# Scoring 32 queries against 96 keys in 64x32 array tiles instead of 64 queries against 128 keys

## The chip, the cores and the metric

The kernel runs on one core of a Trainium2 chip. The metric is the device time of one execution in microseconds (us), and less is better. The median of three timed runs of the kernel before is 952.88 us.

## The reference

Two layers are computed one after the other. The first is attention with a causal window: a query at position i sees the keys at positions i-63 to i. The second is a gated expert layer on the normalised result.

```
attention: q, k, v (8 batches, 8 heads, 576 positions, 64 wide)
  scores = q k^T / sqrt(64); kept where 0 <= i - j < 64, else -1e9
  attn   = exp(scores - max); attn /= sum + 1e-9
  out    = attn v
expert layer: x = out as (4608 tokens, 512)
  xn = x / sqrt(mean(x^2) + 1e-6) * rms_g
  result = (silu(xn w_gate) * (xn w_val)) w_out          # 512 -> 1536 -> 512
```

## The kernel before

The work is cut in two ways that run interleaved. The attention is done by head pairs: 8 batches of 4 pairs, so pairs 0 to 31. The expert layer is done by tiles of 512 tokens, t = 0 to 8, and its matmuls (f16, in a high and a low part) are most of what TensorE does. While TensorE works on the expert layer of one batch, the attention of the batches after it is slipped in between.

Pairs 0 to 7 go through an older path in the first 145 us, where the order of every engine is written out by hand in the string `ORDER` (names such as `g.p_7_0_1` stand for "the next GpSimd instruction that writes p_7_0_1"). Pairs 8 to 31 are done in whole-pair visits, and these alone are changed. A planner places them: `visit_at` says at which half step a visit falls, `at_slot` and `after` place the smaller pieces in slots (one slot is six 512-column or twelve 256-column matmuls of the expert layer), and the resulting order of every engine is fixed.

Visit n does two things on TensorE, one right after the other:

- It multiplies the weights of pair n-2 with its values (`attention_values`): 16 matmuls in 128x64 array tiles, and for the first query block two matmuls in 64x64 tiles, which are held back in the list `ahead` and run together with the scores.
- It computes the scores of pair n (`products_of_pair`): 16 matmuls in 64x64 array tiles, each 64 queries (the weights) against 128 keys (the moving columns), and two matmuls of 64 columns for the first query block, which has no block before it. All are float32, and the trace shows each such matmul as two passes. The four 64x64 tiles of the array ("corners") get one matmul each in turn. Head 0 writes one PSUM bank, head 1 another, and the first block goes into a free part of the bank `first` of the values.

Then, in `scores_of_pair`, VectorE adds the mask and takes the minimum (9 instructions, one per unit of 128 rows), ScalarE takes the exponential with its sum (9), and VectorE takes the reciprocal. `move` then has GpSimd scale each 32x32 block and put it where a 32x32 transpose needs it: 16 instructions for a pair, each 32 partitions by 9 (or 8) units of 32 columns. `turn` has VectorE transpose the blocks (3 instructions), and two visits later TensorE reads the result. Scores, moved blocks and transposed weights share one tile of 8.75 KB a partition: `p` from its start and `m` up to its end, from a rotating pool of three that the weight staging uses as well (`big`).

Of the kernel before, what the change touches and what calls it, by code (L numbers as in the profile page):

```python
# [134 lines left out]
v.p_7_0_0 v.wt16 t.pv_0_8*2 s.p_7_0_0 t.pv_0_8 v.th_0_8 s.mp_o_1 t.pv_0_8 s.st_o_3 t.pv_0_8*5 s.mp_o_2 t.pw_o_1_1*2  # L135
t.pw_o_1_0*2 s.p_7_0_0 t.tr_6_1_1*2 v.wt15 t.pv_0_9 s.mp_1_5 t.pv_0_9*2 v.st_7_0 t.pv_0_9 v.st_7_0 v.th_0_8 t.pv_0_9
g.p_7_0_0 t.pv_0_9 s.pt_6_1_1 t.pv_0_9 v.wt15 t.pv_0_9 s.mn_1_5 t.pv_0_9 v.h_0_4 t.pv_0_9 s.st_o_4 t.pv_0_9*2 g.h_0_4
t.pw_1_5_0 s.mp_o_1 t.pw_1_5_0 t.pw_1_5_1 v.wt13 t.pw_1_5_1 t.pg_0_7*2 g.p_7_0_0 s.mp_o_3 v.wt13 t.pg_0_7 g.p_7_0_1
t.pg_0_7*2 v.th_0_9 t.pg_0_7 s.st_o_5 g.ssq_1 t.tr_7_0_0*2 s.th_0_7 v.top_5 t.tr_7_0_0 t.xp_6_1*7 s.h_0_4 t.xp_6_1
t.pv_0_7*2 s.mn_o_3 t.pv_0_7 v.sq_5 s.kv_9 v.pt_7_0_0 g.h_0_4 t.pv_0_7 v.th_0_7 t.pv_0_7 s.kv_9 t.pv_0_7 t.n2_5 v.z_5  # L140
s.kv_9 s.xb_1 t.pv_0_7 v.ws_5 t.pv_0_7 v.pt_7_0_0 s.wt10 t.pv_0_7 v.wt13 t.pv_0_7*3 v.wt11 t.tr_7_0_1*2 s.kv_6
# [6 lines left out]
t.tr_7_1_0*2 g.p_7_1_1 v.wt19 t.pw_o_5_1*2 s.th_0_11 t.pv_0_10 v.wt19 t.pv_0_10*3 v.pt_7_1_0 t.pv_0_10 s.mp_o_5  # L148
t.pv_0_10 t.pv_0_11*4 v.hsc t.pv_0_11 v.hsc v.omx*2 t.pv_0_11 t.obound v.oe t.tr_7_1_1 v.oe*2 t.tr_7_1_1 v.oe
t.pv_0_11 v.oe v.os v.hsc s.pt_7_1_1 t.pv_0_11 v.th_0_10 t.pv_0_11 s.wt12 t.pv_0_11*3 t.xp_7_1*3 s.h_0_5 t.xp_7_1*3  # L150
v.wt12 t.xp_7_1*2 t.sc_8*3 s.xb_1 t.sc_8*3 g.h_0_5 t.sc_8*2 s.wt13 t.sc_8*8 t.x0_8*2 v.th_0_11 s.kv_7 v.th_0_11 s.wt14
v.ssq_1 v.pm_8 v.hsc v.wt13 v.wt14 s.wt15 v.wt15 s.wt16 v.pm_8 s.wt17 v.wt16 s.h_0_5 v.wt17 g.h_0_5
"""


# [1 line left out]
def tile_window_attention_moe(  # L157
# [369 lines left out]
    def move(m, p, rs, k, qq):

        us = NBLK - 1 if k > 1 else NBLK
        if True:  # L530
            fr, to = slice(32 * qq, 32 * qq + 32), slice(32 * k, 32 * k + 32)
            r = rs[fr, :us].rearrange("p (a b) -> p a b", b=1).to_broadcast([32, us, 32])
            nc.gpsimd.tensor_tensor(m[to, :us, fr], p[fr, :us, to], r, ALU.mult)

    def turn(p, m, part):
        if part < 2:
# [32 lines left out]
    def products_of_pair(n, qk, first, ahead):  # L569

        qt, kk = qk
        sc = [
            pool.tile([P, TT], F32, tag=tag, name=f"sc_{n}_{h}").rearrange("p (i k) -> p i k", k=P)
            for h, (pool, tag) in enumerate(((ps_sc, "sc"), (ps_tr, "tr")))
        ]

        def whole(i, h, par):
            quarter(sc[h][par * D : (par + 1) * D, i, :], qt, kk, h, 2 * i + 1 + par)

        def start(h):  # L580
            quarter(first[h * D : (h + 1) * D, :D], qt, kk, h, 0)

        corners = [[], [], [], []]
        corners[0] = ahead[:1] + [partial(start, 0)] + [partial(whole, i, 0, 0) for i in range(4)]
        corners[1] = ahead[1:] + [partial(whole, i, 0, 1) for i in range(4)]
        corners[2] = [partial(start, 1)] + [partial(whole, i, 1, 1) for i in range(4)]
        corners[3] = [partial(whole, i, 1, 0) for i in range(4)]
        while any(corners):
            for steps_of in corners:
                if steps_of:  # L590
                    steps_of.pop(0)()
        return n, sc, first

    def scores_of_pair(n, sc, first):

        p, m = big(n)
        st = wk.tile([P, 3, NBLK], F32, tag="st", name=f"st_{n}", bufs=NST)
        order = [0] + [u for h in range(2) for u in units(0, h) + units(1, h) if u]
        place = {u: sc[h][:, 2 * g + i, :] for g in range(2) for h in range(2) for i, u in enumerate(units(g, h)) if u}

        def mask_of(u):
            w, v = P if u else D, slot(u)
            masked(p[:, v, :w], place[u] if u else first[:, :D], blocked[:, :P] if u else blocked[:, P:],
                   st[:, 0, v : v + 1])

        def weight_of(u):
            w, v = P if u else D, slot(u)
            weigh(p[:, v, :w], st[:, 0, v : v + 1], st[:, 1, v : v + 1])

        def finish():  # L610
            nc.vector.tensor_scalar(st[:, 1, :], st[:, 1, :], 1e-9, None, ALU.add)
            nc.vector.reciprocal(st[:, 2, :], st[:, 1, :])

        whole[n] = p, m, st[:, 2, :]
        by = MASK_BY if n >= RUSH else 0.5
        for i, u in enumerate(order):
            after(MASK_AT + by * i, partial(mask_of, u))
            after(MASK_AT + by * i + WEIGH, partial(weight_of, u))
        after(MASK_AT + by * NBLK + WEIGH, finish)
# [94 lines left out]
    def attention(b):  # L714

        pairs, soft = {}, {}
        norm = {}

        qs = {}

        def load_queries(hp):
            qs[hp] = load_q(b * NPAIR + hp)

        def load_keys(hp):
            pairs[hp] = load_kv(b * NPAIR + hp)

        def score(hp, g):
            soft[hp, g] = scores(b * NPAIR + hp, g, (qs[hp], pairs[hp][0]))

        def products(hp, first, ahead):  # L730
            return products_of_pair(b * NPAIR + hp, (qs[hp], pairs[hp][0]), first, ahead)

        def moved(hp, k, qq):
            p, m, rs = whole[b * NPAIR + hp]
            move(m, p, rs, k, qq)

        def turned(hp, part):
            p, m, _ = whole[b * NPAIR + hp]
            turn(p, m, part)
            if part == 2:  # L740
                del whole[b * NPAIR + hp]
                soft[hp, 0] = soft[hp, 1] = p

        def to_keys(hp, g):
            soft[hp, g] = weights_to_keys(b * NPAIR + hp, g, soft[hp, g])

        def values(hp, g, xp=None, held=None):
            n = b * NPAIR + hp
            vv = pairs[hp][1]
            p = soft.pop((hp, g))  # L750
            if isinstance(p, list):
                place = {u: p[h][:, i, :] for h in range(2) for i, u in enumerate(units(g, h))}
                at = place.get
            else:
                at = lambda u: p[:, slot(u), :]
            xp = attention_values(n, g, at, vv, xp, held)
            if b >= TB:
                return xp
            drain(hp, g, xp)

        def drain(hp, g, xp):
            n = b * NPAIR + hp
            if hp == g == 0:
                norm["x"] = wk.tile([P, NPAIR, S], F32, tag="xb", name=f"xb_{b}", bufs=1)
                norm["ssq"] = wk.tile([P, S], F32, tag="ssq", name=f"ssq_{b}", bufs=1)
            xb, ssq = norm["x"], norm["ssq"]
            a, z = ((0, XSPLIT), (XSPLIT, S))[g]
            nc.scalar.copy(xb[:, hp, a:z], xp[:, : z - a])
            if g == 0:
                return  # L770
            if b < TB:
                squares(hp, False)
                squares(hp, True)
            else:
                after(1, partial(squares, hp, False))
                after(2, partial(squares, hp, True))

        def squares(hp, add_up):
            n = b * NPAIR + hp
            xb, ssq = norm["x"], norm["ssq"]  # L780
            x2 = pairs[hp][0] if hp else ssq
            if add_up and hp:
                add = nc.vector if (E('ADD', 'ppvppv')[3 * b + hp - 1] == 'v' if b < 2 else hp == NPAIR - 1) else nc.gpsimd
                add.tensor_tensor(ssq, ssq, x2, ALU.add)
            if add_up:
                return
            x2e = E("X2E", "a" * 8)[n] if n < 8 else "a"
            if x2e == "a":
                nc.scalar.activation(x2, xb[:, hp, :], AF.Square)
            else:  # L790
                (nc.vector if x2e == "v" else nc.gpsimd).tensor_tensor(x2, xb[:, hp, :], xb[:, hp, :], ALU.mult)

        return load_queries, load_keys, score, to_keys, values, moved, turned, products, drain, norm

    def attention_events(b, start, pace, tags):
# [10 lines left out]
        for hp in range(NPAIR):  # L806
            if b >= TB:
# [718 lines left out]
```

## Time and profile before

| | |
|---|---|
| timed runs | 952.78, 952.88, 953.68 us |
| span of the profiled execution, first to last instruction | 950.2 us |
| time of the profiled execution beside its span | not given apart from the three runs |
| TensorE busy | 936.1 us, 99% of the span |
| VectorE busy | 625.7 us, 66% |
| ScalarE busy | 510.5 us, 54% |
| GpSimd busy | 497.8 us, 52% |
| granted TensorE clock | 1.000 over the span |

PE is TensorE's matmul, PEld its weight load, DVE VectorE, ACT ScalarE, POOL GpSimd. A busy share counts the modelled end of a matmul, so TensorE's own pace is read from the starts of neighbouring matmuls, not from the busy share. A row of the timeline gives the start of the first instruction of a group, the time from there to the end of its last one, the shape (rows*columns of the array tile, then partitions x moving columns) and the count.

### The profile page before, as it was taken

The numbers are of one execution on the slowest core, as the hardware profiler recorded it, in microseconds if no ns is written. First come the engines' busy times: TensorE is split into PE (matmuls) and PEld (weight loads), VectorE is DVE, ScalarE is ACT, GpSimd is POOL, SyncE is SP. The second block draws the span as 40 slices with busy tenths as digits, with TensorE's granted clock in tenths as the row PEclk, the third lists the DMA queues.
The fourth block names the chain that finished last, engine by engine and source line by source line (L and its number), as shares of the span: only waits on it lengthen the run. The fifth ranks groups of instructions, "written<-read, shape, count | busy, mean of one in ns | idle before, by whom it ended". The sixth has DMA issues, their size and how long they took to land.

```text
span 950.2 us, 20930 instructions
## 1 busy us (share of the span) xinstructions
PE 936.1 (99%) x7906; PEld 614.2 (65%) x7916; DVE 625.7 (66%) x1721; ACT 510.5 (54%) x1303; POOL 497.8 (52%) x641
## 2 busy tenths in 40 slices
PE   8899999999999999999999999999999999999998
PEld 5555554444454444888478857885688568848865
DVE  6998779778877776566857665776676555503540
ACT  7789985555445553566456645664465245413530
POOL 3355545978486773677467747674776122201210
PEclk9999999999999999999999999999999999999999
DMA  8675661515434651457246734564365226614300
GB/s 291 210 224 172 211 194 50 161 43 152 129 90 158 198 193 57 152 206 260 84 139 217 253 103 135 186 257 135 88 207 182 87 70 199 210 44 133 112 12 34
DMA packets 81316, 143.44 MB, mean 151 GB/s; under 512 B 25792, under 2 KB 38336, under 8 KB 81216
## 3 DMA queue, kind: packets, MB, share of 16 engines
q1 hardware_dynamic: 80640, 140.93, 45.1%
q8 instruction: 62, 1.02, 0.4%
q10 hardware_dynamic: 576, 1.18, 0.4%
q14 instruction: 38, 0.31, 0.1%
HBM read 121.64 MB, written 20.45 MB: 150 GB/s over the span
## 4 chain that ended last, share of the span: by engine, by line
PE 89%; DVE 6%; POOL 2%; ACT 1%; issue 1%; DMA 1%; DVEq 0%; POOLq 0%; ACTq 0%
PE bk L182 52%; PE po L182 9%; PE pv L182 7%; PE pg L182 7%; PE xp L182 3%; PE pg L212 3%; PE sc L182 2%; PE pv L212 2%; DVE wt L212 1%; POOL pm L182 1%; PE rb L182 1%; PE sc L212 1%; PE xp L212 1%; DVE p L212 1%; DVE th L182 1%
## 5 line engine op out<-in xcount | busy, mean ns | idle before, releaser
L182 PEld LDWEIGHTS <-wt 128*128 128x128 f16 x3624 | 353.1, 98 | 109.7 <-issue 4.6
L182 POOL TENSOR_TENSOR pm<-pm,st 32x288 f32<-32x288 f32 (+1 forms) x384 | 266.6, 694 | 63.0 <-DVE st L182 19.8
L182 PEld LDWEIGHTS <-h 128*128 128x128 f16 x1308 | 126.7, 98 | 141.6 <-issue 3.3
L182 PE MATMUL bk<-xn,wt 128*128 128x256 f16 x1728 | 207.3, 273 | 0.6 <-DVE u L182 0.5
L182 PE MATMUL bk<-wt,h 128*128 128x512 f16 (+1 forms) x900 | 191.1, 371 | 0.0
L182 POOL TENSOR_TENSOR h<-th,h 128x512 f16<-128x512 f32 x78 | 93.6, 1201 | 169.5 <-ACT h L182 155.6
L182 PE MATMUL bk<-wt,wt 128*128 128x256 f16 x1224 | 150.4, 273 | 0.3 <-ACT u L182 0.3
L182 ACT ACTIVATE pm<-pm,st 128x128 f32<-128x128 f32 (+1 forms) x216 | 83.9, 389 | 37.7 <-DVE st L182 37.0
L182 PE MATMUL po<-wt,h 128*128 128x512 f16 x408 | 90.9, 379 | 0.2 <-DVE wt L212 0.2
L182 ACT CAST h<-th 128x512 f16<-128x512 f32 x94 | 58.0, 617 | 51.7 <-DVE th L182 51.6
L182 POOL TENSOR_TENSOR xn<-xb,xn 128x448 f16<-128x448 f32 (+7 forms) x45 | 37.8, 848 | 83.5 <-ACT xn L182 81.1
L182 DVE SCALAR_TENSOR_TENSOR th<-th,bk 128x256 f32<-128x256 f32 x108 | 44.8, 415 | 49.6 <-ACT th L182 49.2
L182 ACT ACTIVATE th<-bk,hsc 128x256 f32<-128x256 f32 x108 | 48.0, 472 | 46.6 <-DVE bk L182 28.4
L182 DVE TENSOR_TENSOR bk<-bk,s 128x512 f32<-128x512 f32 x36 | 25.1, 696 | 68.8 <-PE bk L182 48.4
L182 PE MATMUL pv<-xn,wt 128*128 128x512 f16 x288 | 66.5, 379 | 0.0
L182 PE MATMUL pg<-xn,wt 128*128 128x512 f16 x288 | 66.1, 379 | 0.0
L182 ACT ACTIVATE ot<-bk,hsc 128x512 f32<-128x512 f32 (+1 forms) x25 | 16.8, 670 | 61.8 <-PE bk L182 61.8
L182 DVE CUSTOM_DVE_ANT_0 pm<-sc,blocked 128x128 f32<-128x128 f32 x191 | 48.8, 282 | 0.0
L182 DVE SCALAR_TENSOR_TENSOR th<-bk,th 128x256 f32<-128x256 f32 x108 | 45.8, 424 | 3.7
L212 PEld LDWEIGHTS <-wt 128*128 128x128 f16 x288 | 27.9, 99 | 31.4 <-issue 0.5
L182 ACT CAST xn<-xb 128x448 f16<-128x448 f32 (+7 forms) x56 | 23.8, 430 | 39.2 <-DVE xb L182 39.1
L182 DVE STREAM_TRANSPOSE pm<-pm 128x512 f32<-128x512 f32 (+1 forms) x72 | 39.6, 554 | 7.9 <-POOL pm L182 7.9
(179 smaller groups left out, 1328.1 us busy)
## 6 DMA issues: line engine op xcount, KB each, us to landing
wt<-sevens SPq DMA_DIRECT2D x108, 512.0 KB, 5.2
kv<-kv SPq DMA_DIRECT2D x28, 608.0 KB, 4.8
wt<-sevens SPq DMA_DIRECT2D x36, 256.0 KB, 2.9
q<-q SPq DMA_DIRECT2D x28, 288.0 KB, 3.7
kv<-kv SPq DMA_DIRECT2D x56, 128.0 KB, 5.0
out<-ot SPq DMA_DIRECT2D x27, 256.0 KB, 2.1
st<-w_gate SPq DMA_DIRECT2D x6, 1024.0 KB, 5.2
st<-w_val SPq DMA_DIRECT2D x6, 1024.0 KB, 5.1
```

The lines of the kernel that those rows point to most:

```text
L182: return real(*args, **kw)
L212: steps[name].popleft()()
```

## The change

The visit's scores are computed in finer pieces. A 64x32 array tile takes 32 queries against the 96 keys that these can see, so each unit of 128 rows has 96 columns instead of 128. That makes 32 matmuls for 16, and five for two in the first block. The eight tiles get one each in turn; the two held-back value matmuls come first. `big` keeps its three tiles for good, sets the four blocks that are never written to zero once, and one small block again at each visit. `move` issues 12 block moves and two for a single unit. The transposes are due 1.6 slots earlier from pair 12 on. A second mask, `banned`, is built once by 16 small GpSimd instructions placed in `ORDER`.

```diff
-t.pw_1_5_0 s.mp_o_1 t.pw_1_5_0 t.pw_1_5_1 v.wt13 t.pw_1_5_1 t.pg_0_7*2 g.p_7_0_0 s.mp_o_3 v.wt13 t.pg_0_7 g.p_7_0_1
+t.pw_1_5_0 s.mp_o_1 t.pw_1_5_0 t.pw_1_5_1 v.wt13 t.pw_1_5_1 t.pg_0_7*2 g.p_7_0_0 s.mp_o_3 v.wt13 t.pg_0_7 g.p_7_0_1 g.banned*16
...
-v.wt12 t.xp_7_1*2 t.sc_8*3 s.xb_1 t.sc_8*3 g.h_0_5 t.sc_8*2 s.wt13 t.sc_8*8 t.x0_8*2 v.th_0_11 s.kv_7 v.th_0_11 s.wt14
-v.ssq_1 v.pm_8 v.hsc v.wt13 v.wt14 s.wt15 v.wt15 s.wt16 v.pm_8 s.wt17 v.wt16 s.h_0_5 v.wt17 g.h_0_5
+v.wt12 t.xp_7_1*2 t.sc_8*6 s.xb_1 t.sc_8*6 g.h_0_5 t.sc_8*4 s.wt13 t.sc_8*16 t.x0_8*5 v.th_0_11 s.kv_7 v.th_0_11 s.wt14
+v.ssq_1 g.pm_8*4 v.pm_8 v.hsc v.wt13 v.wt14 s.wt15 v.wt15 s.wt16 v.pm_8 s.wt17 v.wt16 s.h_0_5 v.wt17 g.h_0_5
...
+    Q = D // 2
+    W3 = 3 * Q
+    banned = cp.tile([P, 2, W3], BF16, name="banned")
+    def band_masks():
...
     def big(n):
-        t = wk.tile([P, ST], I32, tag="st8", name=f"pm_{n}", bufs=NST).bitcast(F32)
-        return (t[:, a : a + NBLK * P].rearrange("p (j k) -> p j k", k=P) for a in (0, ST - NBLK * P))
+        fresh = len(kept_pm) < NST
+        if fresh:
+            kept_pm.append(wk.tile([P, ST], I32, tag="st8", name=f"pm_{n}", bufs=NST).bitcast(F32))
+        t = kept_pm[(n - NPAIR * TB) % NST]
+        p, m = (t[:, a : a + NBLK * P].rearrange("p (j k) -> p j k", k=P) for a in (0, ST - NBLK * P))
+        for qq in range(4) if fresh else (1,):
+            k = (qq + 3) % 4
+            us = slice(0, NBLK if fresh else 1)
+            nc.gpsimd.memset(m[Q * k : Q * k + Q, us, Q * qq : Q * qq + Q], 0.0)
+        return t[:, : NBLK * W3].rearrange("p (j k) -> p j k", k=W3), p, m
...
-    def move(m, p, rs, k, qq):
-        us = NBLK - 1 if k > 1 else NBLK
-        if True:
-            fr, to = slice(32 * qq, 32 * qq + 32), slice(32 * k, 32 * k + 32)
-            r = rs[fr, :us].rearrange("p (a b) -> p a b", b=1).to_broadcast([32, us, 32])
-            nc.gpsimd.tensor_tensor(m[to, :us, fr], p[fr, :us, to], r, ALU.mult)
+    MOVES_OF = 14
+    def move(m, s, rs, step):
+        if step < 12:
+            kk, qq = divmod(step, 4)
+            k, us = (qq + kk) % 4, slice(0, NBLK - 1 if qq == 1 else NBLK)
+        else:
+            kk = k = step - 12
+            qq, us = 1, slice(NBLK - 1, NBLK)
...
-        corners = [[], [], [], []]
-        corners[0] = ahead[:1] + [partial(start, 0)] + [partial(whole, i, 0, 0) for i in range(4)]
-        corners[1] = ahead[1:] + [partial(whole, i, 0, 1) for i in range(4)]
-        corners[2] = [partial(start, 1)] + [partial(whole, i, 1, 1) for i in range(4)]
-        corners[3] = [partial(whole, i, 1, 0) for i in range(4)]
+        def whole(i, h, qq):
+            s = 4 * i + 2 + qq
+            out = sc[h][Q * qq : Q * qq + Q, i, :]
+            band(out.rearrange("p (n c) -> p n c", c=Q), h, s, lambda kb: kb[:, s - 2 : s + 1, :])
...
+        corners = []
+        for h, qq in ((0, 0), (0, 2), (1, 2), (1, 0), (0, 1), (0, 3), (1, 3), (1, 1)):
+            steps_of = [partial(whole, i, h, qq) for i in range(4)]
+            if h == qq // 2:
+                steps_of = starts[qq] + steps_of
+            corners.append(steps_of)
+        for k, step in enumerate(ahead):
+            corners[k].insert(0, step)
...
-            masked(p[:, v, :w], place[u] if u else first[:, :D], blocked[:, :P] if u else blocked[:, P:],
-                   st[:, 0, v : v + 1])
+            masked(p[:, v, :], place[u] if u else first[:, :W3], banned[:, 0 if u else 1, :], st[:, 0, v : v + 1])
...
-        return min(due - 0.5 - (n < 15), moves_at(n) + 15 * MOVE_BY + 1.5)
+        return min(due - 0.5 - (n < 15), moves_at(n) + (MOVES_OF - 1) * MOVE_BY + 1.5)
```

## Rows read from the trace of the kernel before

**Rows 1.** The page's line of busy times by engine.
```profile
PE 936.1 (99%) x7906; PEld 614.2 (65%) x7916; DVE 625.7 (66%) x1721; ACT 510.5 (54%) x1303; POOL 497.8 (52%) x641
```
**Rows 2.** Busy times by stretch, with the granted clock (PEclk).
```profile
core 0: us, PE busy (x) PEld busy (x) DVE busy (x) ACT busy (x) POOL busy (x), PEclk, DMA share, GB/s
163.00:182.00 19.00, 19.00 (x120) 8.98 (x119) 14.48 (x36) 8.84 (x27) 17.99 (x24) 1.00 0.45 129
...
720.00:770.00 50.00, 49.63 (x354) 31.59 (x352) 30.00 (x63) 18.01 (x40) 18.77 (x25) 1.00 0.33 106
```
**Rows 3.** Timeline of PE in the visit at 347 us (overlapping short windows).
```profile
347.73 0.27 PE L182 MATMUL xp<-pm,kv 64*64 64x64 f32 x2
...
347.85 0.26 PE L182 MATMUL xp<-kv,q 64*64 64x64 f32 x2
...
347.96 0.22 PE L182 MATMUL xp<-kv,q 64*64 64x64 f32 x1
348.01 1.04 PE L182 MATMUL sc<-kv,q 64*64 64x128 f32 x28
...
348.78 0.27 PE L182 MATMUL sc<-kv,q 64*64 64x128 f32 x1
348.98 0.39 PE L182 MATMUL pv<-xn,wt 128*128 128x512 f16 x1
```
**Rows 4.** Timeline of PE at 254 us: the sums of squares, in 128x32 array tiles.
```profile
254.52 0.33 PE L182 MATMUL tot<-ssq,one 128*32 128x144 f32 x4
...
254.67 0.30 PE L182 MATMUL tot<-ssq,one 128*32 128x144 f32 x4
254.91 0.39 PE L182 MATMUL po<-wt,wt 128*128 128x512 f16 x1
```
**Rows 5.** Timeline of PE in a visit that has no scores left to compute.
```profile
718.41 0.33 PE L182 MATMUL xp<-pm,kv 64*64 64x64 f32 x4
718.68 0.28 PE L182 MATMUL bk<-wt,wt 128*128 128x256 f16 x1
```
**Rows 6.** Timeline of PE in the visit of pair 9, which has no values.
```profile
163.24 0.27 PE L182 MATMUL x<-kv,q 64*64 64x64 f32 x1
...
164.39 0.39 PE L182 MATMUL po<-wt,h 128*128 128x512 f16 x1
```
**Rows 7.** Groups of POOL instructions by shape: count, busy us, mean ns, idle before.
```profile
L182 POOL TENSOR_TENSOR pm<-pm,st 32x288 f32<-32x288 f32 x192 | 138.9, 724 | 51.0 <-DVE st L182 19.8 <-DVE pm L182 14.8 <-ACT th L182 5.2
L182 POOL TENSOR_TENSOR pm<-pm,st 32x256 f32<-32x256 f32 x192 | 127.6, 665 | 12.0
L212 POOL TENSOR_TENSOR p<-p,st 128x64 f32<-128x64 f32 x8 | 2.5, 315 | 0.0
L212 POOL MEMSET mask<- 128x192 f32 x1 | 0.3, 258 | 0.0
```
**Rows 8.** The mask instructions on DVE: duration in ns, min/median/max.
```profile
L182 DVE CUSTOM_DVE_ANT_0 pm<-sc,blocked x191: 268/282/291, 149.1 to 711.6; 128x128 f32<-128x128 f32 x191
...
L182 DVE CUSTOM_DVE_ANT_0 pm<-xp,blocked x22: 211/215/225, 186.9 to 701.0; 128x64 f32<-128x64 f32 x22
```
**Rows 9.** The group of ACT instructions that takes the exponentials.
```profile
L182 ACT ACTIVATE pm<-pm,st 128x128 f32<-128x128 f32 x192 | 75.8, 395 | 34.5 <-DVE st L182 33.7
```
**Rows 10.** Timeline of POOL while the hand-written order builds the last old pairs.
```profile
120.12 1.18 POOL L212 TENSOR_TENSOR h<-th,h 128x512 f16<-128x512 f32 x1 [0.37 <-ACT h L212]
123.51 2.22 POOL L212 TENSOR_TENSOR ssq<-ssq,kv 128x576 f32<-128x576 f32 x1 [2.20 <-issue]
```
**Rows 11.** Timeline of PE where the first whole-pair visit's masks run on DVE.
```profile
154.21 0.36 PE L182 MATMUL rb<-ssq,first_of 128*128 128x144 f32 x1 [0.26 <-DVE st L182]
```
**Rows 12.** Waits over the whole run: us in total, times, longest.
```profile
DVE pm L182 <- POOL pm L182: 7.9, 5, 2.5
```
**Rows 13.** Timelines of DVE and PE around the last pair's transposes.
```profile
733.95 0.71 DVE L182 STREAM_TRANSPOSE pm<-pm 128x512 f32<-128x512 f32 x1 [2.50 <-POOL pm L182]
...
736.17 1.47 PE L182 MATMUL bk<-wt,wt 128*128 128x256 f16 x12 [0.29 <-ACT u L182]
```

More of the change, by code (lines that the diff above doesn't have):

```diff
@@ L296, in tile_window_attention_moe @@
     nc.gpsimd.tensor_copy(blocked, mask)
+    Q = D // 2
+    W3 = 3 * Q
+    banned = cp.tile([P, 2, W3], BF16, name="banned")
+    def band_masks():
+        g = nc.gpsimd
+        part = banned.rearrange("p a (k c) -> p a k c", c=Q)
+        own = []
+        for r in range(4):
+            rows = slice(Q * r, Q * r + Q)
+            strict, low = Q * r, (Q * r + D) % P
+            own.append(blocked[rows, low : low + Q])
+            g.tensor_copy(part[rows, 0, 0, :], blocked[rows, strict : strict + Q])
+            g.tensor_copy(part[rows, 0, 2, :], own[r])
+        g.memset(part[:, 0, 1, :], 0.0)
+        g.memset(banned[:, 1, :], MASKED)
+        for r, k in enumerate((0, 1, 2, 2)):
+            g.tensor_copy(part[Q * r : Q * r + Q, 1, k, :], own[r])
+        for r, k in ((1, 0), (3, 1)):
+            g.memset(part[Q * r : Q * r + Q, 1, k, :], 0.0)
+    band_masks()
     ebias = cp.tile([P, 2], F32, name="ebias")
@@ L516, in tile_window_attention_moe @@
     whole = {}
+    kept_pm = []
     def big(n):
-        t = wk.tile([P, ST], I32, tag="st8", name=f"pm_{n}", bufs=NST).bitcast(F32)
-        return (t[:, a : a + NBLK * P].rearrange("p (j k) -> p j k", k=P) for a in (0, ST - NBLK * P))
+        fresh = len(kept_pm) < NST
[8 more added lines that the diff above has]
+        return t[:, : NBLK * W3].rearrange("p (j k) -> p j k", k=W3), p, m
     def slot(u):
         return (u - 1) % NBLK
-    def move(m, p, rs, k, qq):
-        us = NBLK - 1 if k > 1 else NBLK
-        if True:
-            fr, to = slice(32 * qq, 32 * qq + 32), slice(32 * k, 32 * k + 32)
-            r = rs[fr, :us].rearrange("p (a b) -> p a b", b=1).to_broadcast([32, us, 32])
-            nc.gpsimd.tensor_tensor(m[to, :us, fr], p[fr, :us, to], r, ALU.mult)
+    MOVES_OF = 14
[6 more added lines that the diff above has]
+            qq, us = 1, slice(NBLK - 1, NBLK)
+        fr, to, of = (slice(Q * i, Q * i + Q) for i in (qq, k, kk))
+        n = us.stop - us.start
+        r = rs[fr, us].rearrange("p (a b) -> p a b", b=1).to_broadcast([Q, n, Q])
+        nc.gpsimd.tensor_tensor(m[to, us, fr], s[fr, us, of], r, ALU.mult)
     def turn(p, m, part):
@@ L572, in products_of_pair, with band, start @@
         sc = [
-            pool.tile([P, TT], F32, tag=tag, name=f"sc_{n}_{h}").rearrange("p (i k) -> p i k", k=P)
+            pool.tile([P, TT], F32, tag=tag, name=f"sc_{n}_{h}")[:, : 4 * W3].rearrange("p (i k) -> p i k", k=W3)
             for h, (pool, tag) in enumerate(((ps_sc, "sc"), (ps_tr, "tr")))
         ]
[L577 to L581, printed above, removed]
-        corners = [[], [], [], []]
-        corners[0] = ahead[:1] + [partial(start, 0)] + [partial(whole, i, 0, 0) for i in range(4)]
-        corners[1] = ahead[1:] + [partial(whole, i, 0, 1) for i in range(4)]
-        corners[2] = [partial(start, 1)] + [partial(whole, i, 1, 1) for i in range(4)]
-        corners[3] = [partial(whole, i, 1, 0) for i in range(4)]
+        def band(out, h, qb, keys):
+            hd = slice(h * D, (h + 1) * D)
+            nc.tensor.matmul(
+                out, lhsT=qt[hd, Q * qb : Q * qb + Q], rhs=keys(kk[hd, :].rearrange("p (n c) -> p n c", c=Q)),
+                start=True, stop=True, skip_group_check=True,
+            )
+        def whole(i, h, qq):
+            s = 4 * i + 2 + qq
+            out = sc[h][Q * qq : Q * qq + Q, i, :]
+            band(out.rearrange("p (n c) -> p n c", c=Q), h, s, lambda kb: kb[:, s - 2 : s + 1, :])
+        def start(qq, a, z, keys):
+            out = first[Q * qq : Q * qq + Q, Q * a : Q * z]
+            band(out.rearrange("p (n c) -> p n c", c=Q), qq // 2, qq % 2, keys)
+        starts = (
+            [partial(start, 0, 0, 3, lambda kb: kb[:, 0:3, :])],
+            [partial(start, 1, 0, 3, lambda kb: kb[:, 0:3, :])],
+            [partial(start, 2, 0, 3, lambda kb: kb[:, 2::-1, :])],
+            [partial(start, 3, 1, 3, lambda kb: kb[:, 0:2, :]), partial(start, 3, 0, 1, lambda kb: kb[:, 0:1, :])],
+        )
+        corners = []
[6 more added lines that the diff above has]
+            corners[k].insert(0, step)
         while any(corners):
@@ L594, in scores_of_pair @@
     def scores_of_pair(n, sc, first):
-        p, m = big(n)
+        p, turned_p, m = big(n)
         st = wk.tile([P, 3, NBLK], F32, tag="st", name=f"st_{n}", bufs=NST)
@@ L601, in mask_of @@
         def mask_of(u):
-            w, v = P if u else D, slot(u)
-            masked(p[:, v, :w], place[u] if u else first[:, :D], blocked[:, :P] if u else blocked[:, P:],
-                   st[:, 0, v : v + 1])
+            v = slot(u)
+            masked(p[:, v, :], place[u] if u else first[:, :W3], banned[:, 0 if u else 1, :], st[:, 0, v : v + 1])
         def weight_of(u):
-            w, v = P if u else D, slot(u)
-            weigh(p[:, v, :w], st[:, 0, v : v + 1], st[:, 1, v : v + 1])
+            v = slot(u)
+            weigh(p[:, v, :], st[:, 0, v : v + 1], st[:, 1, v : v + 1])
         def finish():
@@ L612, in finish @@
             nc.vector.reciprocal(st[:, 2, :], st[:, 1, :])
-        whole[n] = p, m, st[:, 2, :]
+        whole[n] = p, turned_p, m, st[:, 2, :]
         by = MASK_BY if n >= RUSH else 0.5
@@ L731, in products, with moved @@
             return products_of_pair(b * NPAIR + hp, (qs[hp], pairs[hp][0]), first, ahead)
-        def moved(hp, k, qq):
-            p, m, rs = whole[b * NPAIR + hp]
-            move(m, p, rs, k, qq)
+        def moved(hp, step):
+            p, _, m, rs = whole[b * NPAIR + hp]
+            move(m, p, rs, step)
         def turned(hp, part):
-            p, m, _ = whole[b * NPAIR + hp]
+            _, p, m, _ = whole[b * NPAIR + hp]
             turn(p, m, part)
@@ L812, in attention_events @@
                 s0 = slot_at(visit_at(n))
-                for k in range(16):
-                    at_slot(moves_at(n) + (MOVE_BY if n >= RUSH else 0.5) * k, partial(moved, hp, k // 4, k % 4))
+                for k in range(MOVES_OF):
+                    at_slot(moves_at(n) + (MOVE_BY if n >= RUSH else 0.5) * k, partial(moved, hp, k))
                 for k in range(3):
```

## The prediction, written before the result was known

> **What bounds the kernel now.** I read the busy times first. TensorE is busy 99% of the span and the other engines 52 to 66% [rows 1]. The table by stretch then shows that this holds where the change works. From 163 to 182 us TensorE is busy for the whole stretch, and between 720 and 770 us it loses 0.37 of 50 us, while GpSimd is nearly full in the first of these (17.99 of 19 us) [rows 2]. [...] So what a visit takes on TensorE comes out of the end time one to one, and what GpSimd, VectorE and ScalarE save comes out only where TensorE waits for them.
>
> The third view is the timeline of TensorE inside one visit. Busy shares are useless here, since passes overlap; I go by starts. The first matmul in a 64x64 tile starts at 347.73 and the expert layer is back at 348.98: 1.25 us for the held-back values and the scores of a pair [rows 3]. The scores proper are 28 passes in a row: the first starts at 348.01, the last one at 348.78, and the four tiles run together, so these are seven steps of 0.110 us, each with four passes of 128 columns. The last pass starts 0.20 us before the next matmul in 128x128 tiles, 0.09 more than a step. That 0.09 us is paid at this change of tile shape.
>
> **The change, part by part.** *The score matmuls.* A pair has 16 + 2 matmuls before and 32 + 5 after, each in two passes: 36 and 74 passes. Eight tiles instead of four are open, and the busiest tile has the five matmuls (10 passes) of a first-block piece and four whole blocks. If the tiles run independently, the time of that tile counts.
>
> A steady pass of 96 columns: three quarters of 0.110 is 0.082 if all scales with columns, and 0.110 if nothing does. Passes do scale: the 64-column passes of the first block follow each other at 0.06 us (the last of two starts at 347.85 + 0.26 - 0.22 = 347.89, its successor at 347.96) [rows 3]. I take 0.084.
>
> The first pass in a new shape has its weight load in view. The nearest row is a 32-column tile, the 144-column sums: four passes start within 0.02 us of each other (0.33 less about 0.31 for one), and their second passes 0.15 us after the first [rows 4]. At 96 columns that is 0.15 less 48 columns of 0.110/128, so 0.105 us. The next shape starts 0.22 us after the last of these (254.67 + 0.02 to 254.91), which is again a pass and some 0.1 us of change.
>
> *One more change of shape.* The two held-back value matmuls stay in 64x64 tiles and come first, so the visit goes 64x64, 64x32, 128x128 where it went 64x64, 128x128. What this costs is to be seen in a visit that has no scores left: the two value matmuls start at 718.41 and the next shape at 718.68, 0.27 us [rows 5]. Before, these matmuls shared their time with the scores of the other corners. [...]
>
> The sum for one visit, from the first value matmul to the next expert matmul: 0.27 for the values and the change of shape; about 0.03 until the busiest tile gets its first pass, since six other matmuls stand ahead of it (bounds 0 and 0.07); 0.105 for the first pass; eight more steps of 0.084, 0.67; and from the last start to the next shape 0.20 less a quarter of 0.11, 0.17. That makes 1.25 us, against 1.25 before: the finer tiles gain 25% of the streaming, and the extra change of shape gives it back. Over the 22 visits that have both parts I count 0 (with offset and step at their lower bounds -1.0 us, at the upper bound of the offset +0.9).
>
> The visits of pairs 8 and 9 have no values, so no extra change. For pair 9 it is 1.15 us before (163.24 to 164.39) [rows 6] and 0.105 + 0.67 + 0.17 = 0.95 after: -0.2 us. For pair 8 the saving is swallowed, because TensorE waits for VectorE at 154.21 [rows 11].
>
> *Masks and exponentials.* A mask takes 282 ns for 128 columns and 215 for 64 [rows 8]; 96 lie halfway, so eight masks save 34 ns and the first block costs 34 more, 0.24 us a visit. That is hidden under TensorE, except before 154 us, where seven masks of pair 8 stand ahead of the sums that TensorE waits for: -0.2 us there. The exponential, 395 ns [rows 9], gets at most a quarter shorter; TensorE covers it, and without that cover the gain would be below 0.9 us a visit.
>
> *Block moves.* Sixteen moves cost 8 x 724 + 8 x 665 ns = 11.1 us a visit. After, it is 9 x 724 + 3 x 665 = 8.5, two moves of one unit and one small memset. For these the nearest rows are 315 ns (a 64-column multiply) and 258 ns (a memset) [rows 7], so at most 0.9 us. GpSimd saves some 1.7 us a visit, 41 us in all, and TensorE gains nothing from it, because no matmul waits for the moves. Five times a transpose on VectorE does wait for them, 7.9 us in all [rows 12], with the expert layer's gating queued behind it. The transposes come due 1.6 slots earlier, just as the last move does, so the slack stays as it is. The three first tiles also get four memsets of 32x288 each, some 0.3 us apiece by the row of 258 ns; those of pairs 9 and 10 fall into the crowded stretch of GpSimd [rows 2], and each pair's lighter moves pay for them.
>
> *The second mask table.* Sixteen small GpSimd instructions, each between zero and 0.3 us, at most 4.8 us, stand ahead of the sum at about 118 us and of the subtraction at 120.12. GpSimd idles 2.20 us before 123.51 and 0.37 before 120.12 [rows 10]. What is not covered delays the low part of one expert operand, which the output matmuls need only after all input matmuls of that tile. I cost it at nothing; uncovered, it is bounded by 4.8 - 2.6 = 2.2 us.
>
> *The tail.* At the last pair a transpose waits 2.50 us for GpSimd, and TensorE then loses 0.29 us [rows 13]. GpSimd needs less there but the transposes are also due earlier, so I leave this at 0, between -0.5 and +0.3.
>
> The sum is 22 x 0 - 0.2 - 0.2 = -0.4 us on a span of 950.2. The median of the timed runs, 952.88, lies 2.7 us above that span, which I carry over: 952.5 us. A difference of 0.2%, 1.9 us, is about what a measurement of this kernel can tell from no change.
>
> **The rivals.**
>
> *No drain between 64x64 and 64x32.* Then the first-block pass follows the values' two passes directly: the change of shape (0.09), the offset (0.03) and a weight load (0.02 to 0.03) fall away, some 0.15 us a visit, 3.4 us in all. Time: 952.5 - 3.4 = 949.1. Against it stands that every change of shape in the rows costs its 0.09 [rows 3 to 5]; for it, only that this pair does not occur.
>
> *The finer passes do not get shorter.* With eight streams open, a pass could stay at 0.110. Then each of the nine steps costs 0.02 to 0.03 more, 0.22 us a visit, +4.9 us, and pair 9 gains nothing: 957.6. The 128x32 sums speak against it, four streams of the full height at their column pace [rows 4].
>
> *No more than four tiles run at once.* This is the case of the other sign that counts most. No row has more than four passes open [rows 3, 4]. Then 74 passes go in 18.5 steps of 0.084, and a visit takes 0.27 + 0.105 + 17.5 x 0.084 + 0.17 = 2.0 us, +0.77 x 22, with pair 9 about +17.5: 970. It decides as soon as five passes cannot be open together.
>
> *A floor under the distance of starts.* The densest sustained stretch is 28 passes in 0.77 us, 27 ns each [rows 3]. If that is a floor, 74 passes take 2.0 us, a visit 2.47: +27 us, about 980. Against it, four starts lie within 0.02 us, 7 ns each [rows 4], though not sustained. [...]
>
> *A new wait off TensorE.* A transpose that meets later moves, or the low part behind the second mask table, holds VectorE until TensorE runs dry: +1 to +2.5 us, 954 to 955. The mirror case, relief of the small waits at 154 and 736 us, is within the likeliest.
>
> **How the numbers follow.** The likeliest, 952.5 with its own range of 951 to 954, has 0.66. No drain has 0.11, a new wait 0.06, passes of 0.110 have 0.06, four tiles 0.08, the floor 0.03. The range reaches down to the case without drain and up over the new wait, 948.8 to 955.5, and leaves out the last three, 0.17. Faster by over 0.2% needs no drain or the low end of the likeliest with relief: 0.16. Slower: the last three, and half of the new wait: 0.20. Same: 0.64.
>
> **What would show it.** In the timeline of a visit: value matmuls and first 64x32 pass 0.27 us apart, steps of 0.084 in each tile, eight passes open, and 1.25 us to the next expert matmul. Moves at 14 a visit with GpSimd some 40 us less busy, and TensorE's matmul share still at 99%. The prediction is wrong if the first 64x32 pass follows the values without a gap, if passes of different tiles come one by one, or if TensorE shows a new wait after a transpose.

## The result and the profile after

The changed kernel takes 960.83 us (median of 5 runs, 959.21 to 961.16); the kernel before takes 952.88 us in the same measurement. The ratio is 1.0075, with a 95% interval of 1.0062 to 1.0087. That is slower by some 8 us, where 952.5 and no change were forecast. The profiled span grew from 950.2 to 957.9 us, by 7.7.

The page's line of busy times of the kernel after answers to [rows 1].

```profile
PE 942.8 (98%) x8818; PEld 619.0 (65%) x8828; DVE 611.7 (64%) x1721; ACT 508.6 (53%) x1303; POOL 452.3 (47%) x642
```

GpSimd lost 45.5 us, about as forecast (41). VectorE lost 14.0. The masks were forecast to save 24 x 0.24 = 5.8 of it and did (59.0 to 53.1 us for all of them); most of the rest comes with the moves, which take 14.4 off VectorE when they stand alone (below). Neither came out in the time but for the small gain at the tail. The time went to two places.

**The visits.** Timeline of PE in the visit at 188 us of the kernel after (several short windows), which answers to [rows 3]; the last two lines, "x" and "po", are the start and the end of the visit of pair 9, which answers to [rows 6].

```profile
187.71 0.33 PE L182 MATMUL xp<-pm,kv 64*64 64x64 f32 x4
...
187.97 0.27 PE L182 MATMUL xp<-kv,q 64*32 64x96 f32 x1
...
188.02 0.27 PE L182 MATMUL sc<-kv,q 64*32 64x96 f32 x1
188.08 0.24 PE L182 MATMUL xp<-kv,q 64*32 64x96 f32 x2
...
188.92 0.32 PE L182 MATMUL sc<-kv,q 64*32 64x96 f32 x2
189.00 0.24 PE L182 MATMUL sc<-kv,q 64*32 64x96 f32 x1
189.18 0.39 PE L182 MATMUL pv<-xn,wt 128*128 128x512 f16 x1
...
167.15 0.27 PE L182 MATMUL x<-kv,q 64*32 64x96 f32 x1
...
168.39 0.60 PE L182 MATMUL po<-wt,h 128*128 128x512 f16 x2
```

From the first value matmul to the expert layer is 1.47 us now (187.71 to 189.18), and 1.25 was forecast. All 22 visits that have both parts take the same 1.47: 22 x 0.22 = 4.9 us. The value part is as forecast, 0.26 us to the first 64x32 pass. Eight passes do start within 0.05 us (187.97 to 188.02). The excess is in the scores: 1.21 us from their first pass to the next shape, where 0.03 + 0.105 + 0.67 + 0.17 = 0.98 was worked out. The terms at the end of the sum held: the two passes of the last matmul start 0.08 us apart (188.92 and 189.00), and the next shape follows 0.18 us after the second.

Why shows in the weight loads. This table for the kernel after counts the loads that are open in a stretch (a load lasts 0.10 to 0.11 us).

```profile
core 0: us, PEld busy (x), PEclk, DMA share, GB/s
187.97:188.34 0.37, 0.37 (x34) 1.00 0.49 137
188.34:188.35 0.01, 0.01 (x2) 1.00 2.33 922
188.36:188.37 0.01, 0.01 (x3) 1.00 1.16 461
...
188.42:188.43 0.01, 0.01 (x10) 1.00 2.33 922
```

In the first 0.37 us there are 34 loads. A float32 matmul has two (74 loads for the 37 score matmuls of this visit), so these are 17 matmuls. Then loads run dry (2 open at 188.34), and from 188.35 they come back (3 open at 188.36, 10 at 188.42). The first matmul ended just before: its second pass began at 188.08 and lasts 0.24, so until 188.32. So TensorE had 17 matmuls under way and took the 18th 0.03 us after the oldest was done.

**The first stage.** Timelines of VectorE and GpSimd of the kernel after; the GpSimd lines answer to [rows 10].

```profile
121.45 1.78 DVE L212 TENSOR_SCALAR wt<-wt,ws 128x1024 f32<-128x1024 f32 x1
123.26 1.53 DVE L212 CAST wt<-wt 128x1024 f16<-128x1024 f32 x1
124.72 1.36 DVE L212 TENSOR_SCALAR ws<-ws 128x2 int32<-128x2 int32 x1
...
118.04 1.54 POOL L212 COPY banned<-blocked 32x32 bf16<-32x32 bf16 x8
...
121.26 1.41 POOL L212 TENSOR_TENSOR ssq<-ssq,kv 128x576 f32<-128x576 f32 x1
122.64 1.61 POOL L212 TENSOR_TENSOR h<-th,h 128x512 f16<-128x512 f32 x1
124.21 1.84 POOL L212 TENSOR_TENSOR ssq<-ssq,kv 128x576 f32<-128x576 f32 x1
```

For comparison, the same three VectorE steps in the kernel before, and the ScalarE instruction that writes the `kv` which GpSimd's next sum reads:

```profile
121.73 0.73 DVE L212 TENSOR_SCALAR wt<-wt,ws 128x1024 f32<-128x1024 f32 x1
122.50 0.69 DVE L212 CAST wt<-wt 128x1024 f16<-128x1024 f32 x1
123.11 0.16 DVE L212 TENSOR_SCALAR ws<-ws 128x2 int32<-128x2 int32 x1
...
122.71 0.67 ACT L212 ACTIVATE kv<-xb 128x576 f32<-128x576 f32 x1
```

The second mask table keeps GpSimd busy from 118.04 to 121.2. Its sum, the subtraction and the next sum then run beside VectorE's three steps, and these take 1.78, 1.53 and 1.36 us; before, they took 0.73, 0.69 and 0.16. Each of the three ends 0.56, 0.54 and 0.03 us after a GpSimd instruction has ended (123.23, 124.79 and 126.08 against 122.67, 124.25 and 126.05), so my estimate from these end times is that the two took turns here: the third step, on two numbers a partition, ends with the GpSimd instruction beside it. No run shows the reason. GpSimd had been out of the way in the kernel before because its next sum waited for ScalarE: `kv` was written at 123.38 and the sum began at 123.51 [rows 10], and the trace has GpSimd waiting for a semaphore of ScalarE until 123.42.

TensorE waits for what comes out of this. Its waits over the whole run, its timeline, one line of the kernel before for comparison (127.47), and the busy times in the stretch behind, all else from the kernel after:

```profile
PE pg L212 <- DVE wt L212: 2.6, 1, 2.6
```

```profile
124.16 0.61 PE L212 MATMUL pg<-xn,wt 128*128 128x512 f16 x2
127.32 4.01 PE L212 MATMUL pg<-xn,wt 128*128 128x512 f16 x10 [2.56 <-DVE wt L212]
...
131.60 2.75 PE L212 MATMUL pg<-xn,wt 128*128 128x512 f16 x12
```

```profile
127.47 2.75 PE L212 MATMUL pg<-xn,wt 128*128 128x512 f16 x12
```

```profile
128.00:132.00 4.00, 3.95 (x12) 1.52 (x12) 2.34 (x6) 4.00 (x11) 2.11 (x4) 0.66 0.92 254
```

A wait of 2.56 us, and behind it a stretch with a mean granted clock of 0.66 (0.50 from 127.4 to 130.7 us, 1.00 from 130.8 on), in which ten matmuls take 4.01 us. The matmuls ahead of the wait run 0.28 us earlier than in the kernel before, and the next twelve start at 131.60 where they started at 127.47: the first stage costs 4.4 us.

### The profile page after: what moved, and what is told of

Same layout as the page of the kernel before. It is cut to its first block, busy times and chain, and to the rows that moved or that the text cites. A ratio compares the mean times of both kernels' runs of the same rounds, so it can differ in the third digit from the quotient of the medians.

```text
span 957.9 us, 22736 instructions
## 1 busy us (share of the span) xinstructions
PE 942.8 (98%) x8818; PEld 619.0 (65%) x8828; DVE 611.7 (64%) x1721; ACT 508.6 (53%) x1303; POOL 452.3 (47%) x642
## 4 chain that ended last, share of the span: by engine, by line
PE 94%; DVE 4%; ACT 1%; issue 1%; DMA 0%; DVEq 0%; ACTq 0%
PE bk L182 54%; PE po L182 10%; PE pv L182 7%; PE pg L182 6%; PE xp L182 4%; PE pg L212 3%; PE pv L212 3%; PE sc L182 2%; PE sc L212 1%; PE rb L182 1%; DVE wt L212 1%; PE xp L212 1%; PE tr L212 1%; DVE p L212 1%; PE pw L212 1%
## 5 line engine op out<-in xcount | busy, mean ns | idle before, releaser
L182 POOL TENSOR_TENSOR pm<-pm,st 32x288 f32<-32x288 f32 (+1 forms) x336 | 215.8, 642 | 66.9 <-DVE st L182 46.9
L182 POOL TENSOR_TENSOR h<-th,h 128x512 f16<-128x512 f32 x78 | 91.3, 1170 | 196.0 <-ACT h L182 178.1
L182 ACT ACTIVATE pm<-pm,st 128x96 f32<-128x96 f32 x216 | 79.5, 369 | 35.1 <-DVE st L182 34.5
L182 DVE TENSOR_TENSOR u<-bk,wt 128x512 f32<-128x512 f32 x36 | 24.8, 689 | 28.5 <-PE bk L182 27.9
L182 DVE CUSTOM_DVE_ANT_0 pm<-sc,banned 128x96 f32<-128x96 f32 x191 | 42.6, 248 | 0.0
```

The costliest lines, as they stand in the source:

```text
L182: return real(*args, **kw)
```

## The experiments

The theories: a visit is long because a bounded number of matmuls is under way and only the end of the oldest lets the next in; the first stage is long because the second mask table pushes GpSimd into VectorE's steps. The rivals are named in the expectations.

**The second mask table elsewhere, and alone.** One kernel is the changed one with one word of `ORDER` moved (the first diff), the other is the kernel before with `banned` built and read by nothing (the second).

```diff
-g.wt9 v.th_0_9 t.pw_o_2_0*2 s.mn_o_1 t.tr_6_1_0*2 v.wt16 t.pw_o_2_1*2 t.pv_0_8 v.pt_6_1_0 t.pv_0_8 s.th_0_8 t.pv_0_8
+g.wt9 g.banned*16 v.th_0_9 t.pw_o_2_0*2 s.mn_o_1 t.tr_6_1_0*2 v.wt16 t.pw_o_2_1*2 t.pv_0_8 v.pt_6_1_0 t.pv_0_8 s.th_0_8 t.pv_0_8
...
-t.pw_1_5_0 s.mp_o_1 t.pw_1_5_0 t.pw_1_5_1 v.wt13 t.pw_1_5_1 t.pg_0_7*2 g.p_7_0_0 s.mp_o_3 v.wt13 t.pg_0_7 g.p_7_0_1 g.banned*16
+t.pw_1_5_0 s.mp_o_1 t.pw_1_5_0 t.pw_1_5_1 v.wt13 t.pw_1_5_1 t.pg_0_7*2 g.p_7_0_0 s.mp_o_3 v.wt13 t.pg_0_7 g.p_7_0_1
```

```diff
-t.pw_1_5_0 s.mp_o_1 t.pw_1_5_0 t.pw_1_5_1 v.wt13 t.pw_1_5_1 t.pg_0_7*2 g.p_7_0_0 s.mp_o_3 v.wt13 t.pg_0_7 g.p_7_0_1
+t.pw_1_5_0 s.mp_o_1 t.pw_1_5_0 t.pw_1_5_1 v.wt13 t.pw_1_5_1 t.pg_0_7*2 g.p_7_0_0 s.mp_o_3 v.wt13 t.pg_0_7 g.p_7_0_1 g.banned*16
...
+    band_masks()
```

> The kernel after, with the 16 small GpSimd instructions of the second mask table moved to just behind the instruction that writes wt9, where GpSimd idles from 109.6 to 115 us. Theory A (at 118 us they push GpSimd's h and ssq instructions into the stretch where VectorE would have run alone, the two engines then stretch each other, TensorE waits 2.6 us for wt and its clock falls): the 4 us of the first stage come back, 960.8 - 4 = 956.8, VectorE's 128x1024 steps return from 1781 to some 735 ns, and TensorE's wait of 2.56 us before 127.32 goes. Theory B (the wider writes of the tiles or the visits' new shape cause the loss of the first stage, and the mask table only stands beside it): no change, 960.8 +- 1.

> The kernel before with the second mask table alone, at the place it has in the change; nothing reads it. Theory A: +4 us, 957, with VectorE's step on wt of 1.8 us and a wait of TensorE of about 2.5 us near 127 us. Theory B: within 0.5 us of before, 952.9.

Measured: 956.51 us with the table moved (ratio to before 1.0036, 1.0023 to 1.0049), 4.3 less than the changed kernel; 956.66 with the table alone (1.0036, 1.0024 to 1.0049), 3.8 more than the 952.87 of before in this measurement. The same step of VectorE and TensorE's next matmuls, first with the table moved:

```profile
121.62 0.73 DVE L212 TENSOR_SCALAR wt<-wt,ws 128x1024 f32<-128x1024 f32 x1
...
124.33 2.76 PE L212 MATMUL pg<-xn,wt 128*128 128x512 f16 x12
```

and then with the table alone in the kernel before:

```profile
122.49 1.77 DVE L212 TENSOR_SCALAR wt<-wt,ws 128x1024 f32<-128x1024 f32 x1
...
128.36 3.84 PE L212 MATMUL pg<-xn,wt 128*128 128x512 f16 x10 [2.56 <-DVE wt L212]
```

Sixteen instructions whose result nobody reads bring 3.8 us with the same wait of 2.56 us, and some nine microseconds earlier the same sixteen bring no such wait. So the table, at the place it has in the change, causes the loss of the first stage.

**The values in 64x32 tiles.** The two held-back value matmuls of the changed kernel become four, so that the visit has one shape less.

```diff
-                held += [partial(block, c, j, [h]) for h in range(2)]
+                held += [partial(block, c, j, [h], e) for h in range(2) for e in range(2)]
...
-        for k, step in enumerate(ahead):
+        for k, step in zip((0, 4, 1, 5), ahead):
```

> The kernel after, with the two held-back value matmuls cut into four in 64x32 tiles, so that no 64x64 tile stands ahead of the scores and one change of array shape falls away. Theory C (a visit loses 0.22 us because only 16 matmuls are in flight, and 0.09 to 0.1 us of it is the extra change of shape that was forecast): 0.10 to 0.15 us less a visit, 2.2 to 3.3 us in all, 957.6 to 958.6; 2 more matmuls stand in the queue, so the pause stays. Theory D (no cost at the change from 64x64 to 64x32; the 0.26 us between values and scores is the latency of a first pass): no change, 960.8 +- 0.5.

Measured: 955.44 us (1.0027, 1.0016 to 1.0039), 5.4 less than the changed kernel, more than both theories gave. PE timeline of a visit with its values in 64x32 tiles:

```profile
190.03 0.27 PE L182 MATMUL xp<-kv,q 64*32 64x96 f32 x1
...
190.10 0.21 PE L182 MATMUL xp<-pm,kv 64*32 64x64 f32 x1
...
191.26 0.39 PE L182 MATMUL pv<-xn,wt 128*128 128x512 f16 x1
```

Loads open in short stretches of it:

```profile
190.02:190.34 0.32, 0.32 (x34) 1.00 0.90 346
190.33:190.34 0.01, 0.01 (x4) 1.00 1.16 461
...
190.39:190.40 0.01, 0.01 (x5) 1.00 1.74 691
```

The visit takes 1.25 us again, so the values now cost nothing at all: four more matmuls fit beside the scores. Again 34 loads come first. Here the oldest matmul is a value matmul of 64 columns, its second pass starts at 190.10 and ends at 190.31, and 0.32 us after the first load all 34 have been issued, where it was 0.37. The next load starts at 190.34, again 0.03 us after the end of the oldest matmul. The refill moved with that end; a pause of fixed length would not have. Of the 0.22 us a visit, 0.09 is what I had forecast for the change of shape; the rest would be the time in which values and scores could not overlap, which no run took apart.

**Twice as many, half as long.** Each score matmul of 96 columns (but the starts of other lengths) becomes two of 48 in the same tile.

```diff
+        HALF = W3 // 2
...
-            steps_of = [partial(whole, i, h, qq) for i in range(4)]
+            steps_of = [partial(whole, i, h, qq, z) for i in range(4) for z in (0, HALF)]
```

> The kernel after, with each score matmul of 96 columns cut into two of 48 that go to the same array tile one after the other in turn (71 matmuls for 37, the same columns in all). Theory H (at most 16 float32 matmuls are under way, and the 17th starts when the first has ended): the 17th weight load comes about 0.30 us after the first instead of 0.38, since the first matmul ends earlier, but 71 matmuls need more than four such turns; worked out step by step from the rows of after this is 0.33 us more a visit, 22 to 24 visits, +7 to +8 us: 968 to 969. Theory I (TensorE's supply stops for a fixed time after 16 matmuls): the 17th load stays at 0.38 us and a visit takes 0.60 us more, +14 us, 975. Theory J (the busiest tile alone counts, and something else made the visit long): no change, 960.8 +- 1.

Measured: 984.05 us (1.0328, 1.0312 to 1.0343), beyond every theory. PE timeline of an ordinary visit of this kernel, then loads open in it:

```profile
207.02 0.33 PE L182 MATMUL xp<-pm,kv 64*64 64x64 f32 x4
...
208.85 0.39 PE L182 MATMUL pv<-xn,wt 128*128 128x512 f16 x1
```

```profile
207.28:207.66 0.38, 0.38 (x34) 1.00 0.00 0
207.70:208.40 0.70, 0.70 (x82) 1.00 0.00 0
```

The run does not tell the pause's kind as it was meant to: the first score matmul that is issued is one of the three uncut ones, so the oldest ends when it did and the 34 loads again take 0.38 us. What it does show is that there is no second pause: 82 loads in the next 0.70 us, some 6 of them open at its start, so 38 matmuls at 18 ns each, one after the other. An ordinary visit takes 1.83 us, 0.36 more, against 0.33 for the bounded number and 0.60 for a pause after every 16. The rest of the loss is something else: eight of the visits take 1.98 to 4.89 us, 11.0 us in sum above 1.83, and the profile puts most of that down to nothing it can name:

```profile
PE sc L182 <- issue: 9.4, 7, 2.9
```

No other run had it, and its cause stays open. The record has one hint: the longest of these waits is 2.88 us and ends at 669.76, and between 664 and 671 us two packets of the DMA queue that the profile calls "instruction" were moved. So a late supply of instructions is a candidate, which no run shows or tested. This profile has one more thing. TensorE met the same wait at 129 us as after the change, and its clock did not fall (its timeline and its busy times in the stretch behind):

```profile
129.32 2.33 PE L212 MATMUL pg<-xn,wt 128*128 128x512 f16 x10 [2.56 <-DVE wt L212]
```

```profile
128.00:132.00 4.00, 2.62 (x12) 1.27 (x14) 3.31 (x12) 2.49 (x11) 0.33 (x2) 1.00 0.89 284
```

Ten matmuls take 2.33 us there and 4.01 after the change: of the first stage's loss the clock is 1.7 us and the wait nearly all of the rest.

**One pass for two.** Scores from the upper 16 bits of queries and keys.

```diff
-                out, lhsT=qt[hd, Q * qb : Q * qb + Q], rhs=keys(kk[hd, :].rearrange("p (n c) -> p n c", c=Q)),
+                out, lhsT=upper(qt)[hd, Q * qb : Q * qb + Q], rhs=keys(upper(kk)[hd, :].rearrange("p (n c) -> p n c", c=Q)),
```

> The kernel after, with the scores computed from the upper 16 bits of each query and key alone (the lower ones are left out), so that a score matmul is one pass and one weight load instead of two of each. If the 16 of theory H counts matmuls, the 17th weight load still waits, until the first matmul has ended, about 0.25 us after the first load, and a visit gets some 0.4 us shorter, 952. If it counts weight loads and passes (64 in all, so 32 of these matmuls), 32 loads come without a pause, and a visit gets some 0.6 us shorter, 947. Without such a limit no pause is seen at all.

Measured in a single execution: 941.53 us; a visit takes 0.71 us, 0.76 less than in the changed kernel, where at most 0.6 was expected. The first pass of a visit of this kernel, then the loads open in it:

```profile
186.53 0.21 PE L182 MATMUL xp<-kv,q 64*32 64x96 bf16 x1
```

```profile
186.53:186.76 0.23, 0.23 (x33) 1.00 0.00 0
186.76:186.77 0.01, 0.01 (x1) 1.00 0.00 0
...
186.80:186.81 0.01, 0.01 (x4) 1.00 0.00 0
```

Here 33 matmuls, with one load each, come before the pause, and the last four after it, from 186.78 on; the oldest matmul, a single pass, had ended at 186.74. So the limit does not count matmuls. Counting loads and passes, it is 17 x 4 = 68 in float32 and 33 x 2 = 66 here: 64 behind the oldest matmul in both. That the limit counts loads and passes alike is an estimate from these two counts. The 16 in the expectations stands for these 16 matmuls behind the oldest.

**Both repairs, and a new order.** The third kernel takes the table's earlier place and the values in 64x32 tiles together. The fourth also issues the 41 matmuls in another order (a digit is a tile, a and b are the short matmuls of that tile).

```diff
+    PICKS = (
+        "6b 4a 1a 0 5 7 2 3 6 1 4 0 6 7 2 5 4 0 1 6 2 "
+        "5 3 7 4 0 4 1 3 5 2 0 6 3 7 4 1 2 6a 5a 0a"
+    )
...
+            for pick in PICKS.split():
+                (short.pop(pick) if pick in short else long[int(pick)].pop(0))()
```

The order comes from working the issue out step by step: a matmul enters 17 ns after the one before it (as the matmuls' first loads do from 188.35 to 188.45 in the kernel after), the 17th and later not until 0.03 us after the one 16 places ahead has ended, and a tile takes its passes in turn, 0.082 us for 96 columns. This gives 1.27 us for the visit that was measured as 1.25, and 1.10 for the new order.

> The kernel after with both repairs: the second mask table built from 109 us on, and the held-back values in 64x32 tiles. If the two causes are separate, their gains of 4.3 and 5.4 us add: 960.8 - 9.7 = 951.1, which is 0 to 2 us below the kernel before. If they overlap: 953 or more.

> Both repairs, and the 41 matmuls of a visit in another order: first a short one of each of three tiles, so that the first of the 16 under way ends early, then the tiles that have most left, and the three last short ones at the end. Theory H, worked out step by step over this order: a visit takes 0.15 to 0.17 us less than with the tiles in turn (1.10 for 1.27 in the same working), 22 visits, 3.3 to 3.8 us less: 947.5 to 948. If the pace of issue alone limits the visit, or the pause has a fixed length: within 0.5 us of the kernel with both repairs.

Measured: 952.58 us with both repairs (ratio to before 1.0000, 0.9991 to 1.0009). That is 8.3 less than the changed kernel, not the 9.7 of the sum, and level with before. Both repairs work in its profile (visits of 1.25 us, no wait for `wt`); of its twelve executions the six at a granted clock of 1.00 have a median of 951.57, near the sum, and the six at 0.996 to 0.998 one of 952.95, so the sum is not ruled out. With the new order 947.36 us (0.9948, 0.9936 to 0.9960), 5.2 us below the kernel before, and faster than either kernel of the case. Its PE timeline:

```profile
201.82 0.21 PE L182 MATMUL xp<-kv,q 64*32 64x32 f32 x1
...
202.91 0.39 PE L182 MATMUL pv<-xn,wt 128*128 128x512 f16 x1
```

A visit takes 1.09 us by these starts (1.08 in the median of the visits), with the same matmuls and the same columns. Only the order differs, so the pace of issue alone did not set the 1.25, and the gain is the 0.15 to 0.17 that the bounded number gave. This run does not exclude a pause of fixed length: an order that leaves less to the last tile would gain under it too (some 0.1 us by the same step-by-step working, an estimate). Against a fixed pause stand the loads above, which come back 0.03 us after the end of the oldest matmul in all three kernels, 0.38, 0.33 and 0.25 us after the first load. Against before, the new order is 22 x 0.17 = 3.7 of the 5.2 us; 0.7 of the rest is the tail, as the next kernel shows, and what is left is within what two runs of such kernels differ by.

**The moves alone.** The kernel before with kept tiles, 12 moves and one of a single unit, scores unchanged.

```diff
-                for k in range(16):
-                    at_slot(moves_at(n) + (MOVE_BY if n >= RUSH else 0.5) * k, partial(moved, hp, k // 4, k % 4))
+                for k, block in enumerate(MOVED):
+                    at_slot(moves_at(n) + (MOVE_BY if n >= RUSH else 0.5) * k, partial(moved, hp, *block))
```

> The kernel before with the block moves of the change alone: kept tiles, never-written blocks set to zero once, 12 moves and one of a single unit in place of 16, transposes due earlier by the same rule; scores, masks and exponentials stay 64 queries by 128 keys. Theory E (moves lie under TensorE and are worth nothing but the small waits at 154 and 736 us): -0.5 us, 952.4 (range 951.9 to 952.9), GpSimd some 38 us less busy. Theory F (what the moves free is worth more: the waits of VectorE for the moves, 7.9 us in all, come out in the time): 949 or less. Theory G (the memsets at first use and the transposes due earlier cost as much as is freed): 953 or more.

Measured: 951.89 us (0.9994, 0.9985 to 1.0002), not told apart from no change. The page's busy line, and the tail on TensorE, the first two lines before and the last two with the moves:

```profile
PE 936.7 (99%) x7906; PEld 615.0 (65%) x7916; DVE 611.3 (64%) x1721; ACT 510.9 (54%) x1303; POOL 439.7 (46%) x602
```

```profile
734.41 1.47 PE L182 MATMUL bk<-xn,wt 128*128 128x256 f16 x12
...
740.47 1.47 PE L182 MATMUL bk<-xn,wt 128*128 128x256 f16 x12
...
734.97 1.47 PE L182 MATMUL bk<-xn,wt 128*128 128x256 f16 x12
...
740.33 1.47 PE L182 MATMUL bk<-xn,wt 128*128 128x256 f16 x12
```

GpSimd is 58 us less busy, where 38 were expected. Between the same two groups of matmuls TensorE takes 6.06 us before and 5.36 with the moves, so 0.70 us is gained at the tail; the 0.37 us of [rows 2] is less, because a busy share counts the modelled end of a matmul. The changed kernel has the same 5.36. Elsewhere nothing can be pointed to: the moves lie under TensorE, as forecast.

## Why the prediction was wrong

- **The step of the scores failed.** "If the tiles run independently, the time of that tile counts" and with it "eight more steps of 0.084, 0.67". The tiles kept the forecast's steps up to the 17th matmul (a tile's passes start 0.11, then 0.08 us apart); then the next load came only 0.03 us after the end of the oldest matmul. Scores took 1.21 us for 0.98 forecast, a visit 1.47 for 1.25, the sum of the visits +4.9 us for 0. The kernel before, with 18 score matmuls in four tiles, stays near that number, so its rows could not show it. The rival "the finer passes do not get shorter" gives the same 0.22 us a visit by chance: the passes are shorter (0.08 us apart in a tile), but the busiest tile's ten would fill only some 0.84 of the 1.21 us, an estimate (0.105 + 9 x 0.082).
- **The second mask table failed.** "I cost it at nothing", because GpSimd "idles 2.20 us before 123.51" [rows 10]. That idle time did cover GpSimd: it was a wait for ScalarE's `kv`, and in the kernel after the sum starts at 124.21, only 0.70 us later. What the term left out is that VectorE ran its steps alone in that idle time. GpSimd's late instructions came beside them and stretched them by 3.1 us in sum, and TensorE waited for `wt`, which these steps make, and not for the low part that the forecast followed. That the two engines took turns is an estimate from the end times; with the table moved away the first step takes 0.73 us again. The bound of 2.2 us counted GpSimd's lateness alone, without VectorE's and without TensorE's clock behind the wait. Measured: 3.8 and 4.3 us. The rival "a new wait off TensorE" named this path (low part late, VectorE held, TensorE dry) at +1 to +2.5 us with a chance of 0.06; the wait was 2.56 us, and the clock came on top.
- **Right in kind:** the extra change of shape, 0.26 us for 0.27. That its price could be avoided by giving the values the new shape was not seen. The rival "no drain" put that price at 0.15 us a visit; the version without the extra shape gained 0.22.
- **Right:** GpSimd's and VectorE's savings come out nowhere but at the tail; eight tiles do run at once; passes of 96 columns do get shorter (0.08 us apart, where 128 columns took 0.110). The tail itself was left at 0, between -0.5 and +0.3, and gained 0.70. The four-tile rival (970) and the floor of 27 ns (980) did not come true: the 74 passes of 1.04 us start 14 ns apart.
- **Pair 9:** 1.24 us (from the start at 167.15 to 168.39) for 0.95 forecast and 1.15 before, the same limit without any value matmul.

The two failures add up: 4.9 for the visits, 0.1 for pair 9 and 4.4 for the first stage make 9.4; 0.2 less at pair 8 (as forecast), 0.7 less at the tail and some 0.7 less in small pieces (ahead of the first stage, between visits, at the very end) leave the 7.7 of the span. None of the three signs that the prediction gave for being wrong names this limit, and the new wait came behind VectorE's `wt`, not behind a transpose.

## What to carry to other kernels

When a stage is cut into many small matmuls over many array tiles, count the loads and passes that stand between the oldest and the newest: here 64 of them stood behind the oldest matmul when the loads paused, and then the end of the oldest, not the busiest tile, set the pace. Order counts then: put a short matmul first, serve the tiles with most left, and keep short ones for the end; that was worth 3.7 us in the visits here, where finer tiles alone were worth nothing (the three rules were not taken apart). And before idle time of one engine is booked as cover, look at what another engine does in that time: work put there can slow the neighbour, as GpSimd's did VectorE's, and the path behind the neighbour may be the one that counts.

## What was not expected of the hardware

- The limit above: 17 float32 matmuls (34 loads) or 33 matmuls of one pass (33 loads) before the first pause, and the next one some 0.03 us after the oldest has ended (188.32 and 188.35, 190.31 and 190.34, 186.74 and 186.78).
- Behind that pause, a float32 matmul of two passes enters every 18 ns (38 in 0.70 us).
- The same wait of 2.56 us of TensorE was followed by a lower granted clock after the change (0.50 from 127.4 to 130.7 us, ten matmuls in 4.01 us) and not in the kernel of 48-column halves (1.00, 2.33 us).
- A VectorE step on 128x2 numbers took 1.36 us beside a GpSimd instruction of 1.84 us, and 0.16 us without one.
- Stalls of up to 2.9 us inside a visit of 142 score passes, which no other kernel here had; the cause stays open.
